# Feed-forward matmuls as two 64-column tiles, and each engine's order set by a plan made at build time

## The chip, the core and the metric

The kernel runs on one core of one Trainium2 chip. The metric is the device time in microseconds, the median of several executions. A profile of one execution gives the span from the first to the last instruction, and the busy time, waits and transfers of each engine: TensorE (PE, its weight loads as PEld), VectorE (DVE), ScalarE (ACT), GpSimd (POOL, which here only issues loads) and SyncE (SP, which issues the stores).

## The reference

Attention with a squared relu instead of a softmax, for 8 batches of 12 heads, 448 positions and 64 dimensions, and behind it one gated feed-forward layer on the 3,584 rows that come out:

```python
scores = scale * np.matmul(q, k.transpose(0, 1, 3, 2))
attn = np.maximum(scores, 0.0) ** 2 / S
attn_out = np.matmul(attn, v)
x = attn_out.transpose(0, 2, 1, 3).reshape(B * S, H * D)     # 3584 x 768
g = x @ w_gate                                               # 768 x 1536
gelu = 0.5 * g * (1.0 + erf(g * inv_sqrt2))
out = (gelu * (x @ w_val)) @ w_out                           # 1536 x 768
```

Inputs and output are float32 in memory; the kernel multiplies in bf16 and accumulates in float32.

## The kernel before

The work is cut by batch (8) and, in the attention, by pairs of heads (6 a batch, 48 in all). One pair n goes through four steps:

- `transposes(n)`: 16 PE transposes of 112 x 64 blocks of q and k into one PSUM bank (tile `tps`), in two 64-column halves of the array, one head in each; DVE copies the bank to `qkT`.
- `scores(n, half)`: two units of the four that a pair has. A unit is two matmuls side by side, each on 64 rows of the array, into a two-bank tile `sp`; ACT takes the relu into `rl`, DVE squares it into `attnT`.
- `values(n)`: 8 matmuls, two 64-column halves side by side, accumulate the pair's output in tile `op`; DVE scales it into `xT`.
- The batch's `xT` is full when its sixth pair is through.

The feed-forward works on a whole batch: `gate_value(b, fc)`, for 12 chunks of 128 of the 1,536 columns, accumulates six 448-column matmuls for the gate and six for the value, each on the full 128 x 128 array. ACT takes the gelu of the first, DVE multiplies it with the second into `uT`. `out_half(sb, t, g)` accumulates 12 matmuls of 384 columns for 128 rows of the output and half its width, ACT copies them to `osb`, and behind the second half SP stores them. Batches go two by two through `uT`, so an even batch has 6 such halves behind its chunks and an odd one 8.

The eight PSUM banks are split: one for `tps`, one for `op`, four for two `sp` tiles, two for the feed-forward's tile `ff`.

The order on every engine is the order in which the code is written. First come 48 warm-up matmuls of four tile shapes on a zero tile. Then stands the whole attention of batch 0, item by item: values of the pair before, transposes of the pair after, both score halves. From there on the feed-forward items of batch b are written one after the other, and the 12 attention items of batch b + 1 are dealt out between them at even shares of an estimated cost (`due`). POOL issues the loads: batch 0 in 18 pieces of one pair, then the weights with batch 1 in three parts between them, then each later batch whole, as soon as its buffer is free.

Of the kernel before, what the change touches and what calls it, by code (L numbers as in the profile page):

```python
# [8 lines left out]


@with_exitstack
def kernel(
# [10 lines left out]
    nc = tc.nc  # L23
# [9 lines left out]
    NP = B * NPAIR  # L33
    d_model, d_ff = moe_w_gate.shape
# [6 lines left out]
    WOG = 3  # L41

# [9 lines left out]
    apool = ctx.enter_context(tc.tile_pool(name="apool", bufs=10))  # L52
# [9 lines left out]

# [4 lines left out]


    def warm_up():
        full = psF.tile([128, 512], f32, name="ff", tag="F")  # L70
        cols = psF.tile([128, 512], f32, name="ff", tag="F")
        rows = psS.tile([128, 2, 512], f32, name="sp", tag="S")
        quad = psS.tile([128, 2, 512], f32, name="sp", tag="S")

        def mm(o, l, r, at):
            nc.tensor.matmul(o, l, r, start=True, stop=True, tile_position=at)  # L76

        for shape in ("full", "full", "cols", "full", "rows", "full", "quad", "cols", "rows"):
            for i in range(3):
                if shape == "full":  # L80
                    mm(full[:, :], warm[:, 0:128], warm[:, :], (0, 0))
                elif shape == "cols":
                    for j in range(2):
                        o = slice(64 * j, 64 * j + 64)
                        mm(cols[o, :], warm[:, o], warm[:, :], (0, 64 * j))
                elif shape == "rows":
                    for j in range(2):
                        r = slice(64 * j, 64 * j + 64)
                        mm(rows[:, j, :], warm[r, 0:128], warm[r, :], (64 * j, 0))
                else:  # L90
                    for j in range(4):
                        r = slice(64 * (j % 2), 64 * (j % 2) + 64)
                        o = slice(64 * (j // 2), 64 * (j // 2) + 64)
                        mm(quad[o, j % 2, :], warm[r, 0:64], warm[r, :],
                           (64 * (j % 2), 64 * (j // 2)))
# [5 lines left out]
          for i in range(FC // WOG)]  # L101

    def load_w12(i):
        cols = slice(i * WCH, (i + 1) * WCH)
        for wt, src in ((wg[i], moe_w_gate), (wv[i], moe_w_val)):
            nc.gpsimd.dma_start(
                wt[:, :, :], src[:, cols].rearrange("(c p) f -> p c f", p=128))

    def load_wo(i):
        rows = slice(i * WOG * 128, (i + 1) * WOG * 128)  # L110
        nc.gpsimd.dma_start(
            wo[i][:, :, :], moe_w_out[rows, :].rearrange("(c p) f -> p c f", p=128))

    batch = {}

    def alloc_batch(b):
        batch[b] = [qkv.tile([P, H, SC, D], bf16, name=n, tag=n) for n in ("q16", "k16", "v16")]

    def load_heads(b, h0, h1):
        for t, src in zip(batch[b], (q, k, v)):  # L120
            nc.gpsimd.dma_start(  # L121
                t[:, h0:h1, :, :],
                src[b, h0:h1].rearrange("h (p c) d -> p h c d", c=SC))


    qkT = {}
    att = {}
    xT = {}

    def transposes(n):  # L130
        b, pr = divmod(n, NPAIR)
        q16, k16, _ = batch[b]
        tps = psT.tile([128, 2, SC, 128], bf16, name="tps", tag="T")
        for c in range(SC):
            for i, src in enumerate((q16, k16)):
                for j in range(2):
                    rows = slice(64 * j, 64 * j + 64)
                    nc.tensor.transpose(tps[rows, i, c, 0:P], src[:, 2 * pr + j, c, :],  # L138
                                        ident[0:P, 0:P], tile_position=(0, 64 * j))
        qkT[n] = qk_pool.tile([128, 2, S], bf16, name="qkT", tag="qkT")  # L140
        nc.vector.tensor_copy(  # L141
            qkT[n].rearrange("d i (c p) -> d i c p", p=P), tps[:, :, :, 0:P])

    def scores(n, half):
        t = qkT[n]
        for c in (2 * half, 2 * half + 1):
            sp = psS.tile([128, 2, 512], f32, name="sp", tag="S")
            for j in range(2):
                rows = slice(64 * j, 64 * j + 64)
                nc.tensor.matmul(sp[0:P, j, 0:S], t[rows, 1, c * P:(c + 1) * P],  # L150
                                 t[rows, 0, :], start=True, stop=True,
                                 tile_position=(64 * j, 0))
            rl = rpool.tile([P, 2, S], bf16, name="rl", tag="rl")
            nc.scalar.activation(rl[:, :, :], sp[0:P, :, 0:S], AF.Relu)  # L154
            a = apool.tile([P, 2, S], bf16, name="attnT", tag="attnT")
            nc.vector.tensor_tensor(a[:, :, :], rl[:, :, :], rl[:, :, :], op=ALU.mult)  # L156
            att[n, c] = a

    def values(n):
        b, pr = divmod(n, NPAIR)  # L160
        v16 = batch[b][2]
        if pr == 0:
            xT[b] = xpool.tile([128, KC, S], bf16, name="xT", tag="xT")
        op = psO.tile([128, S], f32, name="op", tag="O")
        for c in range(SC):
            a = att.pop((n, c))
            for j in range(2):
                rows = slice(64 * j, 64 * j + 64)
                nc.tensor.matmul(op[rows, :], v16[:, 2 * pr + j, c, :], a[:, j, :],  # L169
                                 start=(c == 0), stop=(c == SC - 1),  # L170
                                 tile_position=(0, 64 * j))
        nc.vector.tensor_scalar_mul(xT[b][:, pr, :], op[:, :], scalar1=out_scale)  # L172

    def attn_item(m):
        n, half = divmod(m, 2)
        if half == 0:
            if n > 0:
                values(n - 1)
            if n + 1 < NP:
                transposes(n + 1)  # L180
            if n < NP:
                scores(n, 0)
        elif n < NP:
            scores(n, 1)


    uT = {}

    def gate_value(b, fc):
        x = xT[b]  # L190
        if b % 2 == 0 and fc == 0:
            uT[b // 2] = upool.tile([128, FC, 2 * S], bf16, name="uT", tag="uT")
        i, o = divmod(fc * 128, WCH)
        ps = []
        for w in (wg[i], wv[i]):
            pt = psF.tile([128, 512], f32, name="ff", tag="F")
            for dc in range(KC):
# [121 lines left out]
```

## Time and profile before

| | |
|---|---|
| median of 3 executions | 487.95 us (486.2 to 487.95) |
| the profiled execution | 487.95 us, its span 486.2 us |
| weight and input loads (POOL's queue) | 23.60 MB, 36.4% of 16 DMA engines |
| output stores (SP's queue) | 11.01 MB, 7.3% |
| score matmuls (L150) | 384, 396 ns each, 5.4 us of PE idle before them in all |
| relu on ACT (L154) | 192, 915 ns each |
| square on DVE (L156) | 192, 625 ns each |

A matmul's row in the profile lasts longer than its turn on PE, since matmuls are pipelined: what one costs is read from the start of one to the start of the next. Where two halves run side by side, a pair has one turn. The mean clock column tells which share of its full clock TensorE was granted.

### The profile page before, as it was taken

The numbers are of one execution on the slowest core, as the hardware profiler recorded it, in microseconds if no ns is written. First come the engines' busy times: TensorE is split into PE (matmuls) and PEld (weight loads), VectorE is DVE, ScalarE is ACT, GpSimd is POOL, SyncE is SP. The second block draws the span as 40 slices with busy tenths as digits, with TensorE's granted clock in tenths as the row PEclk, the third lists the DMA queues.
The fourth block names the chain that finished last, engine by engine and source line by source line (L and its number), as shares of the span: only waits on it lengthen the run. The fifth ranks groups of instructions, "written<-read, shape, count | busy, mean of one in ns | idle before, by whom it ended". The sixth has DMA issues, their size and how long they took to land.

```text
span 486.2 us, 8140 instructions
## 1 busy us (share of the span) xinstructions
PE 472.3 (97%) x3408; PEld 240.0 (49%) x3408; DVE 236.2 (49%) x385; ACT 238.8 (49%) x346; POOL 48.7 (10%) x67
## 2 busy tenths in 40 slices
PE   8788999999999999999999999999999999999996
PEld 2333444554555554555555554454455544555553
DVE  0666556445643466546563456536564466532210
ACT  1555654564545455555454645545455555452221
POOL 9744200100010000100010000100000000000000
PEclk9655999999999999999999999999999999999999
DMA  8999990950028600933009600555002200021013
GB/s 109 178 196 198 205 200 12 147 111 12 1 34 167 101 1 1 128 93 49 1 4 178 111 11 2 75 119 76 1 0 66 67 0 1 2 67 32 1 32 98
DMA packets 48501, 35.13 MB, mean 72 GB/s; under 512 B 1872, under 2 KB 44880, under 8 KB 48464
## 3 DMA queue, kind: packets, MB, share of 16 engines
q0 software_dynamic: 43984, 23.60, 36.4%
q1 hardware_dynamic: 4480, 11.01, 7.3%
q8 instruction: 26, 0.43, 0.4%
q14 instruction: 11, 0.09, 0.1%
HBM read 47.19 MB, written 11.01 MB: 120 GB/s over the span
## 4 chain that ended last, share of the span: by engine, by line
PE 94%; ACT 3%; DVE 2%; issue 1%; ACTq 0%
PE ff L198 46%; PE ff L218 23%; PE sp L150 10%; PE op L169 8%; PE tps L138 4%; ACT rl L154 2%; DVE attnT L156 2%; PE ff L76 1%; PE sp L76 0%; DVE qkT L141 0%; ACT osb L221 0%; DVE warm L64 0%; ACTq L154 0%
## 5 line engine op out<-in xcount | busy, mean ns | idle before, releaser
L154 ACT ACTIVATE rl<-sp 112x896 bf16<-112x896 f32 x192 | 165.1, 915 | 121.7 <-PE sp L150 121.7
L156 DVE TENSOR_TENSOR attnT<-rl 112x896 bf16<-112x896 bf16 x192 | 120.1, 625 | 103.1 <-ACT rl L154 103.1
L198 PE MATMUL ff<-xT,wg 128*128 128x448 bf16 x576 | 126.3, 356 | 0.0
L198 PE MATMUL ff<-xT,wv 128*128 128x448 bf16 x576 | 124.6, 352 | 0.0
L218 PE MATMUL ff<-wo,uT 128*128 128x384 bf16 x672 | 114.2, 326 | 0.0
L205 DVE TENSOR_TENSOR uT<-gel,ff 128x448 bf16<-128x448 bf16 x96 | 59.7, 622 | 76.7 <-PE ff L198 74.1
L218 PEld LDWEIGHTS <-uT 128*128 128x128 bf16 x672 | 63.8, 98 | 48.7 <-issue 8.1
L198 PEld LDWEIGHTS <-wg 128*128 128x128 bf16 x576 | 51.6, 98 | 63.0 <-issue 21.2
L198 PEld LDWEIGHTS <-wv 128*128 128x128 bf16 x576 | 56.4, 98 | 52.8 <-issue 0.4
L203 ACT ACTIVATE gel<-ff 128x448 bf16<-128x448 f32 x96 | 52.4, 546 | 57.5 <-PE ff L198 57.5
L150 PE MATMUL sp<-qkT 64*112 64x448 bf16 x384 | 62.1, 396 | 5.4 <-ACT rl L154 5.4
L221 ACT COPY osb<-ff 128x384 f32<-128x384 f32 x56 | 26.8, 479 | 63.3 <-PE ff L218 63.3
L169 PE MATMUL op<-attnT,v 112*64 112x448 bf16 x384 | 51.9, 382 | 2.0 <-DVE attnT L156 2.0
L172 DVE TENSOR_SCALAR xT<-op 128x448 bf16<-128x448 f32 x48 | 30.0, 625 | 38.4 <-PE op L169 38.4
L141 DVE COPY qkT<-tps 128x896 bf16<-128x896 bf16 x48 | 29.6, 617 | 11.4 <-PE tps L138 10.6
L169 PEld LDWEIGHTS <-v 112*64 112x64 bf16 x384 | 19.3, 112 | 30.9 <-issue 22.7
L150 PEld LDWEIGHTS <-qkT 64*112 64x112 bf16 x384 | 19.6, 131 | 30.0 <-issue 25.9
L121 POOL DMA_DIRECT2D q<-in_q_dram x15 | 12.0, 799 | 172.8 <-PE tps L138 169.3
L138 PE MATMUL tps<-ident,q 112*64 112x112 bf16 x384 | 27.0, 224 | 0.7 <-DVE qkT L141 0.7
L138 PE MATMUL tps<-ident,k 112*64 112x112 bf16 x384 | 27.0, 223 | 0.0
L138 PEld LDWEIGHTS <-q 112*64 112x64 bf16 x384 | 22.5, 117 | 4.3 <-issue 0.8
L138 PEld LDWEIGHTS <-k 112*64 112x64 bf16 x384 | 21.9, 118 | 3.9
(17 smaller groups left out, 52.5 us busy)
## 6 DMA issues: line engine op xcount, KB each, us to landing
q<-in_q_dram POOLq DMA_DIRECT2D x6, 672.0 KB, 7.0
k<-in_k_dram POOLq DMA_DIRECT2D x6, 672.0 KB, 10.3
v<-in_v_dram POOLq DMA_DIRECT2D x6, 672.0 KB, 8.1
out_dram<-osb SPq DMA_DIRECT2D x8, 336.0 KB, 3.2
wg<-in_moe_w_gate_dram POOLq DMA_DIRECT2D x6, 384.0 KB, 13.2
wv<-in_moe_w_val_dram POOLq DMA_DIRECT2D x6, 384.0 KB, 12.8
wo<-in_moe_w_out_dram POOLq DMA_DIRECT2D x4, 576.0 KB, 15.7
out_dram<-osb SPq DMA_DIRECT2D x8, 288.0 KB, 2.6
```

What stands on the lines that cost most here:

```text
L138: nc.tensor.transpose(tps[rows, i, c, 0:P], src[:, 2 * pr + j, c, :], ident[0:P, 0:P], tile_position=(0, 64 * j))
L141: nc.vector.tensor_copy(qkT[n].rearrange("d i (c p) -> d i c p", p=P), tps[:, :, :, 0:P])
L150: nc.tensor.matmul(sp[0:P, j, 0:S], t[rows, 1, c * P:(c + 1) * P], t[rows, 0, :], start=True, stop=True, tile_position=(64 * j, 0))
L154: nc.scalar.activation(rl[:, :, :], sp[0:P, :, 0:S], AF.Relu)
L156: nc.vector.tensor_tensor(a[:, :, :], rl[:, :, :], rl[:, :, :], op=ALU.mult)
L169: nc.tensor.matmul(op[rows, :], v16[:, 2 * pr + j, c, :], a[:, j, :], start=(c == 0), stop=(c == SC - 1), tile_position=(0, 64 * j))
L172: nc.vector.tensor_scalar_mul(xT[b][:, pr, :], op[:, :], scalar1=out_scale)
L198: nc.tensor.matmul(pt[:, 0:S], w[:, dc, o:o + 128], x[:, dc, :], start=(dc == 0), stop=(dc == KC - 1))
L203: nc.scalar.activation(gel[:, :], pt[:, 0:S], AF.Gelu)
L205: nc.vector.tensor_tensor(uT[b // 2][:, fc, base:base + S], gel[:, :], ps[1][:, 0:S], op=ALU.mult)
L218: nc.tensor.matmul(rp[:, 0:OGS], u[:, fc, cols], wo[i][:, o, g * OGS:(g + 1) * OGS], start=(fc == 0), stop=(fc == FC - 1))
L221: nc.scalar.copy(osb[0][:, g * OGS:(g + 1) * OGS], rp[:, 0:OGS])
```

## The change

Six things change together.

1. Every gate, value and output matmul is issued as two matmuls with 64 columns of weights each (`mm_cols`), at the tile positions (0, 0) and (0, 64), the form that the transposes and the values already have. They write the two halves of the partitions of one bank. The two score units of a half keep their form of two 64-row tiles.
2. The code no longer emits instructions as it goes. It makes lists of operations with an engine, a cost and dependencies, and `run_plan` emits them in the order in which they come ready: PE and POOL in the order of a list sorted by planned times, ACT and DVE whichever of the first 48 waiting operations could start first.
3. The planned times put batch 0 at 60 to 12 us ahead of the first feed-forward matmul, with the values of a pair 4.2 units behind its last scores; later batches are spread evenly over the feed-forward of the batch before and end 6 us ahead of it (`LEAD`).
4. Transposes, values and feed-forward share four banks (`psF`), with the two two-bank `sp` tiles beside them.
5. The warm-up is 10 pairs of one shape instead of 48 matmuls of four.
6. The three parts of batch 1 are loaded earlier among the weights, and there are 12 `attnT` buffers instead of 10.

The multiplications, the evictions and the bytes moved are the same.

```diff
+def run_plan(queues, pools, arrivals):
...
+        for e, ops in queues.items():
+            if at[e] < len(ops):
+                r = ready(ops[at[e]])
+                if r is not None:
+                    key = (max(r, free[e]), 0)
...
+        for e, ops in pools.items():
+            mine = None
+            for op in ops[:48]:
+                r = ready(op)
+                if r is not None:
+                    key = (max(r, free[e]), op.prio)
...
+        op.emit()
...
-    psT = ctx.enter_context(tc.tile_pool(name="psT", bufs=1, space=bass.MemoryType.PSUM))
-    psS = ctx.enter_context(tc.tile_pool(name="psS", bufs=2, space=bass.MemoryType.PSUM))
-    psO = ctx.enter_context(tc.tile_pool(name="psO", bufs=1, space=bass.MemoryType.PSUM))
-    psF = ctx.enter_context(tc.tile_pool(name="psF", bufs=2, space=bass.MemoryType.PSUM))
+    psS = ctx.enter_context(tc.tile_pool(name="psS", bufs=SB, space=bass.MemoryType.PSUM))
+    psF = ctx.enter_context(tc.tile_pool(name="psF", bufs=FB, space=bass.MemoryType.PSUM))
...
+    def mm_cols(o, lhsT, rhs, start, stop):
+
+        for j in range(2):
+            h = slice(64 * j, 64 * j + 64)
+            nc.tensor.matmul(o[h], lhsT[:, h], rhs, start=start, stop=stop,
+                             tile_position=(0, 64 * j))
...
+    def ring_dep():
+        return [ring[-FB]] if len(ring) >= FB else []
...
+            op = Op("PE", cost, emit, [t_op[n], relu_op.get(u - SB)],
+                    lag=0.25 if u < u1 - 1 else 0.15)
...
+        op = Op("PE", 0.77, emit, [head_op[b, pr, 2], *(sq_op[SC * n + c] for c in range(SC)),
+                                   *ring_dep()], lag=0.24)
...
-                nc.tensor.matmul(pt[:, 0:S], w[:, dc, o:o + 128], x[:, dc, :],
-                                 start=(dc == 0), stop=(dc == KC - 1))
+                mm_cols(pt[:, 0:S], w[:, dc, o:o + 128], x[:, dc, :],
+                        dc == 0, dc == KC - 1)
...
-            nc.tensor.matmul(rp[:, 0:OGS], u[:, fc, cols],
-                             wo[i][:, o, g * OGS:(g + 1) * OGS],
-                             start=(fc == 0), stop=(fc == FC - 1))
+                mm_cols(rp[:, 0:OGS], u[:, fc, t * TT:(t + 1) * TT],
+                        wo[i][:, o, g * OGS:(g + 1) * OGS], fc == 0, fc == FC - 1)
...
+    LEAD = 6.0
+    for b in range(B):
+        if b == 0:
+            lo, hi = -60.0, -12.0
+        elif b == 1:
+            lo, hi = -8.0, starts[1] - LEAD
+        else:
+            lo, hi = starts[b - 1] - LEAD, starts[b] - LEAD
+        step = (hi - lo) / (SC * NPAIR)
+        for pr in range(NPAIR):
+            n = NPAIR * b + pr
+            work.append((lo + (SC * pr) * step - max(3.0, 2 * step), 1, add_transposes, (n,)))
+            work.append((lo + (SC * pr + SC - 1) * step + max(4.5, (4.2 if b == 0 else 3.3) * step), 2, add_values, (n,)))
+        for u in range(0, SC * NPAIR, SB):
+            work.append((lo + (u + SB - 1) * step, 3, add_scores,
+                         (SC * NPAIR * b + u, SC * NPAIR * b + u + SB)))
+    work.sort(key=lambda w: w[:2])
```

How the instructions now stand is seen at three places. The first is DVE's queue at the start, in batch 0, where PE's scores and values wait for it. A row is one operation, or several in a row with their count; `qkT` is the copy of a pair's transposes, `attnT` a square, `xT` the scaled values. Before:

```order
L141 COPY qkT<-tps 128x896 x2
L156 TENSOR_TENSOR attnT<-rl 112x896 x4
L172 TENSOR_SCALAR xT<-op 128x448
L141 COPY qkT<-tps 128x896
L156 TENSOR_TENSOR attnT<-rl 112x896 x4
```

and in the changed kernel:

```order
L205 COPY qkT<-ff 128x896 x2
L233 TENSOR_TENSOR attnT<-rl 112x896 x4
L205 COPY qkT<-ff 128x896
L233 TENSOR_TENSOR attnT<-rl 112x896 x3
L262 TENSOR_SCALAR xT<-ff 128x448
L233 TENSOR_TENSOR attnT<-rl 112x896
L205 COPY qkT<-ff 128x896
```

The first scaled values stand behind seven squares instead of four, and the third pair's transposes are copied ahead of them: the values of a pair have moved one pair back.

The second place is PE's queue at the end of a value accumulation, where the values of a pair follow it (batch 1, while batch 0 is in the feed-forward). `wv` and `v` are weights loaded into the array, and the shape is that of the output. Before:

```order
L198 LDWEIGHTS wv_113
L198 MATMUL ff<-xT,wv_113 128x448
L169 LDWEIGHTS v_127
L169 MATMUL op<-attnT,v_127 64x448
L169 LDWEIGHTS v_127
```

and in the changed kernel:

```order
L136 LDWEIGHTS wv_106
L136 MATMUL ff<-xT,wv_106 64x448
L136 LDWEIGHTS wv_106
L136 MATMUL ff<-xT,wv_106 64x448
L257 LDWEIGHTS v_340
L257 MATMUL ff<-attnT,v_340 64x448
```

The last accumulation step is now two matmuls of 64 output partitions, and the values behind it have the same shape and the same tile positions.

The third place is POOL's queue behind the 18 loads of batch 0, where the first weights and the first part of batch 1 (four heads, two pairs: 112 x 4 x 256) are issued. Before:

```order
L106 DMA wg_106<-in_moe_w_gate_dram 128x6x256
L106 DMA wv_112<-in_moe_w_val_dram 128x6x256
L106 DMA wg_107<-in_moe_w_gate_dram 128x6x256
L106 DMA wv_113<-in_moe_w_val_dram 128x6x256
L121 DMA q_125<-in_q_dram 112x4x256
L121 DMA k_126<-in_k_dram 112x4x256
```

and in the changed kernel:

```order
L160 DMA wg_100<-in_moe_w_gate_dram 128x6x256
L160 DMA wv_106<-in_moe_w_val_dram 128x6x256
L175 DMA q_316<-in_q_dram 112x4x256
L175 DMA k_334<-in_k_dram 112x4x256
L175 DMA v_340<-in_v_dram 112x4x256
L160 DMA wg_101<-in_moe_w_gate_dram 128x6x256
L160 DMA wv_107<-in_moe_w_val_dram 128x6x256
L160 DMA wg_102<-in_moe_w_gate_dram 128x6x256
```

The first part of batch 1 has moved ahead of the second pair of weights; its second part now stands behind the third pair instead of the fourth, its third part behind the fourth instead of behind half of `w_out`.

More of the change, by code (lines that the diff above doesn't have):

```diff
@@ L66 @@
     ctx.enter_context(tc.manual_schedule())
[L69 to L95, printed above, removed]
+    def mm_cols(o, lhsT, rhs, start, stop):
[3 more added lines that the diff above has]
+                             tile_position=(0, 64 * j))
+    PE, ACT, DVE, POOL = [], [], [], []
+    arrivals = {}
     wg = [wpool.tile([128, KC, WCH], bf16, name=f"wg{i}", tag=f"wg{i}") for i in range(NW)]
@@ L144, in scores @@
[L144 to L157, printed above, removed]
@@ L159, in values @@
-    def values(n):
-        b, pr = divmod(n, NPAIR)
[L161 to L172, printed above, removed]
@@ new lines, in load_heads, with emit @@
+    def load_heads(b, h0, h1, deps=((), (), ())):
+        for i, (name, src) in enumerate((("q16", q), ("k16", k), ("v16", v))):
+            def emit(i=i, name=name, src=src):
+                if (b, i) not in batch:
+                    batch[b, i] = qkv.tile([P, H, SC, D], bf16, name=name, tag=name)
+                nc.gpsimd.dma_start(
+                    batch[b, i][:, h0:h1, :, :],
+                    src[b, h0:h1].rearrange("h (p c) d -> p h c d", c=SC))
+            op = load(4 * (h1 - h0) * S * D, emit, deps[i])
+            for pr in range(h0 // 2, h1 // 2):
+                head_op[b, pr, i] = op
@@ L292 @@
+    work.sort(key=lambda w: w[:2])
+    add_warm_up(10)
+    for _, _, fn, args in work:
+        fn(*args)
+        b, pr = divmod(args[0], NPAIR)
+        if fn is add_values and pr == NPAIR - 1 and b + 2 < B:
+            n = args[0]
+            load_heads(b + 2, 0, H, ((t_op[n],), (t_op[n],), (o_op[n],)))
+    run_plan({"PE": PE, "POOL": POOL}, {"ACT": ACT, "DVE": DVE}, arrivals)
 _INS = ['q', 'k', 'v', 'moe_w_gate', 'moe_w_val', 'moe_w_out']
```

302 lines of the change are left out of this document (196 added, 106 removed).

## The prediction, made before the changed kernel was run

> **What bounds the kernel now.** I read the page first, for the busiest engine and the chain that ended last; then a table by stage; then the chain and the timeline inside the two stages that differ.
>
> ```profile
> span 486.2 us, 8140 instructions
> PE 472.3 (97%) x3408; PEld 240.0 (49%) x3408; DVE 236.2 (49%) x385; ACT 238.8 (49%) x346; POOL 48.7 (10%) x67
> PE 94%; ACT 3%; DVE 2%; issue 1%; ACTq 0%
> ```
>
> PE is 94% of the chain, so only two things can shorten this kernel: less PE time, or fewer microseconds in which PE isn't the bound. The table by stage (stretch, its length, then busy time of PE, PEld, DVE, ACT, POOL with counts, granted clock, DMA share, GB/s) says where the latter lie.
>
> ```profile
> 6.60:16.85 10.25, 7.44 (x82) 3.04 (x83) 3.75 (x6) 3.34 (x4) 10.25 (x16) 1.00 1.30 165
> 16.85:50.95 34.10, 28.86 (x188) 13.66 (x188) 21.21 (x34) 19.07 (x23) 16.54 (x22) 0.50 1.41 195
> 51.00:438.50 387.50, 387.50 (x2887) 198.53 (x2885) 202.82 (x332) 204.66 (x299) 16.28 (x18) 1.00 0.37 63
> 438.58:481.50 42.92, 42.92 (x240) 23.33 (x240) 8.08 (x13) 9.89 (x19) 0.00 (x0) 1.00 0.13 37
> 481.50:486.20 4.70, 0.02 (x1) 0.00 (x0) 0.00 (x0) 0.48 (x1) 0.00 (x0) 0.82 0.28 84
> ```
>
> From 51 to 481.5 us PE is never idle, at full clock; DVE and ACT are busy half the time. The last 4.7 us are the last eviction and its store. Before 51 us PE has only 188 matmuls in 34 us, at clock 0.50. The chain there (start, length, what):
>
> ```profile
> 28.73 0.58 PE op L169 x2
> 29.32 0.75 PE tps L138 x16
> 30.06 0.57 PE sp L150 x2
> 31.47 0.92 ACT rl L154
> ...
> 34.04 0.64 DVE attnT L156
> 34.72 0.58 PE op L169 x2
> ...
> 48.95 3.40 PE ff L198 x12
> ```
>
> and ACT's row of the timeline in the same loop:
>
> ```profile
> 36.65 3.35 ACT L154 ACTIVATE rl<-sp 112x896 bf16<-112x896 f32 x4 [2.63 <-PE sp L150]
> ```
>
> One head pair takes 34.72 − 28.73 = 5.99 us, and ACT idles 2.63 us in each: its next scores stand on PE behind values that wait for the last square of the same pair. So batch 0 runs as a serial loop PE, ACT, DVE, PE, and the first feed-forward matmul starts at 48.95. Call that point F.
>
> **After F.** I write T for the transposes of a pair, S for two score units, V for the values of a pair, G and U for a gate and a value accumulation, R for one output half. The steady rows of the timeline (start, length, then what; the length holds the latency of the last one, so costs are read from start to start), and two of the chain at the end, where nothing disturbs:
>
> ```profile
> 201.73 2.12 PE L218 MATMUL ff<-wo,uT 128*128 128x384 bf16 x12
> 203.79 0.95 PE L169 MATMUL op<-attnT,v 112*64 112x448 bf16 x8
> 204.57 0.22 PE L138 MATMUL tps<-ident,q 112*64 112x112 bf16 x2
> ...
> 205.06 0.59 PE L150 MATMUL sp<-qkT 64*112 64x448 bf16 x4
> 205.58 4.07 PE L218 MATMUL ff<-wo,uT 128*128 128x384 bf16 x24
> 209.58 0.58 PE L150 MATMUL sp<-qkT 64*112 64x448 bf16 x4
> ...
> 221.06 1.30 PE L198 MATMUL ff<-xT,wg 128*128 128x448 bf16 x6
> 222.20 1.30 PE L198 MATMUL ff<-xT,wv 128*128 128x448 bf16 x6
> 223.43 0.95 PE L169 MATMUL op<-attnT,v 112*64 112x448 bf16 x8
> ```
>
> ```profile
> 438.58 27.35 PE ff L198 x144
> 465.92 15.61 PE ff L218 x96
> ```
>
> Undisturbed, a 448-column matmul costs 27.35/144 = 0.190 us and a 384-column one 15.61/96 = 0.163. G to U is 1.14 us (6 x 0.19), but U to V is 1.23 and R12 to V 2.06 instead of 1.95: a change between the full array and 64-column tiles costs some 0.10. T after V follows without such a step (0.78 for four pairs of V, 0.195 a pair), T to S has one (0.49 for 16 transposes, 8 x 0.05 plus 0.10), S takes 0.52, R24 after it 4.00 instead of 3.90. Per pair there are five changes: into V, into and out of S, twice.
>
> **The change, part by part.** (1) *64-column tiles in G, U and R.* V, T, G, U and R now share one tile shape, so the change into V goes: 0.10, and some 0.02 that V's first pair loses (0.78 − 4 x 0.19), 0.12 a pair. 42 of the 48 V stand behind F: **−5.0 us**. The four changes around S stay. Every full matmul becomes two half-width ones, 1,824 pairs. V's pairs cost 0.195 with that first loss in it, 0.19 without; I take 0.19, so **0**. At 0.195 the 1,152 pairs of G and U cost 5.8 us and the 672 of R some 3.4: upper end +9. Below 0 nothing, since the columns streamed are the same.
>
> This needs the weight loads to hide. Full loads already do. A half one is no shorter (the groups' last numbers ahead of the second bar are mean ns):
>
> ```profile
> L198 PEld LDWEIGHTS <-wg 128*128 128x128 bf16 x576 | 51.6, 98 | 63.0 <-issue 21.2
> L169 PEld LDWEIGHTS <-v 112*64 112x64 bf16 x384 | 19.3, 112 | 30.9 <-issue 22.7
> ```
>
> Two of 112 ns in turn would be 0.224 us, more than the 0.19 of the pair above them, yet V and T run at 0.19 and 0.05 a pair with two loads each: the loads overlap. The Trainium skill speaks against the change here: "TensorEngine Tiling (Array Packing)", Restrictions and Gotchas, excludes Fast Weight Load under column tiling, and "TensorE: Matmul & The Clock Gate", Part 3, lets a load overlap a running matmul only in another row group, while both tiles here use all rows. The 112 ns for half the columns fit the first; T's pairs of 0.05 us disagree with the second. By these pages the loads would show and the time would be that of the third rival.
>
> (2) *The head.* The new order puts V one pair behind its scores, so nothing on PE waits for a square just made. What is late next: ACT and DVE at once. ACT's four relus take 3.35 us, (3.35 − 0.92)/3 = 0.81 apart. DVE, back to back:
>
> ```profile
> 67.34 0.62 DVE L205 TENSOR_TENSOR uT<-gel,ff 128x448 bf16<-128x448 bf16 x1 [2.05 <-PE ff L198]
> 67.88 0.62 DVE L172 TENSOR_SCALAR xT<-op 128x448 bf16<-128x448 f32 x1
> 68.42 0.61 DVE L141 COPY qkT<-tps 128x896 bf16<-128x896 bf16 x1
> ```
>
> That is 0.54 an operation, six a pair: 3.24 us, the same as four relus. The rows of the start, and of three loads with the us from issue to landing:
>
> ```profile
> 1.19 5.55 PE L76 MATMUL ff<-warm 128*128 128x512 bf16 x15 [1.19 <-DVE warm L64]
> 2.42 0.67 POOL L121 DMA_DIRECT2D k<-in_k_dram  x1
> k<-in_k_dram POOLq DMA_DIRECT2D x1, 112.0 KB, 3.7
> 21.09 0.83 POOL L106 DMA_DIRECT2D wv<-in_moe_w_val_dram  x1 [1.40 <-DMA wg<-in_moe_w_gate_dram]
> wv<-in_moe_w_val_dram POOLq DMA_DIRECT2D x1, 384.0 KB, 13.2
> 48.10 0.77 POOL L111 DMA_DIRECT2D wo<-in_moe_w_out_dram  x1 [1.25 <-DMA wg<-in_moe_w_gate_dram]
> wo<-in_moe_w_out_dram POOLq DMA_DIRECT2D x1, 576.0 KB, 18.0
> ```
>
> The warm row holds 12 slots of 512 columns in 5.55 us, 0.46 each; ten end at 5.8, and the first k lands at 2.42 + 3.7 = 6.1. From the first transpose to the first relu I allow 2.4 us: 8.5. Then 24 relus: 19.4 us if neither engine ever misses a beat, 21.6 at 0.90; I take 0.90, as two equally loaded engines fed in order will miss some: 30.1. Behind the last relu stand a square, V, its copy and the scores of the next pair: 2.5. F = 32.6. But the eighth pair's transposes stand only 3 us behind F (G, U, one S) and need a k that is loaded after the third weight pair. The bytes ahead of it are those that landed with wv at 21.09 + 13.2 = 34.3, plus two 224 KB loads, 2.3 us at 195 GB/s: 36.6. So F counts as no earlier than 33.6 whatever the engines do. I take **34.5**, a gain of 14.4. The lower end is 33.6; the upper is the first rival. One more S stands ahead of F, which is 0.6 less behind it. The 2 us after F at half clock, which lost 1.0, go if the head keeps full clock.
>
> (3) *Load order.* Weights 2 to 6 land up to 3.5 us later (three 224 KB loads); they are wanted one pair every 4.5 us from F on. All w_out has the same bytes ahead as before and lands at 66.1; the first R is 37 us behind F, at 71. Batch 2 (two 672 KB loads, 73) is wanted 41 us behind F, at 75. **0**, with 2 to 5 us of cover; if F came earlier the cover would go first. SP's stores are not moved.
>
> (4) *Four shared banks, planned ACT and DVE queues.* Each buffer is taken again four accumulations later, over 2 us, against evictions of 0.6 us on engines half idle: **0**, up to +5 (0.1 a pair) if an eviction stands behind squares.
>
> Sum: −14.4 − 5.0 − 0.6 − 1.0 = −21.0. The profiled execution took 487.95 us, the span and 1.75 around it, and is the median of the runs shown: **467.0**.
>
> **Rivals.** *Cold head.* Clock 0.50 held although PE was busy 28.9 of 34.1 us. If the short warm-up, ending before the first load lands, doesn't bring full clock, or the new head can't keep it, PE bounds the head: per pair at half clock T 0.75, V and S 1.5 each (four 448-column pairs, by the 0.75 of eight 112-column ones), four changes of 0.18: 4.5 against 3.6. F near 38.3, the 1.0 lost again: **472**. For it: the old stage stayed cold 85% busy. Against: the new order packs PE fuller. The Trainium skill ("TensorE: Matmul & The Clock Gate", HAM oscillation) wants only that no idle gap exceeds about 3.4 us, by which the head would be warm; here the clock fell at 16.85 although PE idles only 2.8 us in all of the 10.25 before, so the rule doesn't decide.
>
> *No gain behind F.* G to V costs what U to V costs now, because 128 and 112 rows differ (never adjacent in this trace), or the shared banks take 5 us: **472**.
>
> *Weights show.* The slower end: half-width pairs above 0.19 us, in G, U and R, by loads or by the doubled stream of instructions. All the gain is gone at 21/1,824 = 11.5 ns a pair; two exposed loads of 112 ns would be +409, **876**. Against: V and T, 1,152 matmuls already in this form.
>
> *The change doesn't do what it says.* The head stays serial through some wait of the new queues: only the steady gain, **482**.
>
> **How the numbers follow.** Forecast 0.50, cold head 0.26, no gain behind F 0.11 (with both 477), pairs at 0.195 (476) 0.05, serial head 0.03, weights showing 0.04 with nearly all of it slower, 0.01 even. A measurement of this kernel tells about 0.5% from no change, so faster 0.95, same 0.01, slower 0.04. The range must take in both clocks and the ends 33.6 and +5: 463.5 to 475.
>
> **What would show it.** In the changed profile: a first feed-forward matmul near 34.5 at clock 1.00 (cold head: 0.50, at 38); relus under 0.95 us apart before it; the eighth pair's transposes waiting for a load of k or not at all; G and U at 1.14 us with V behind at no extra; PE idle 0 from F to 42.9 us before the last eviction. Half-width pairs above 0.195 us, or PE waiting for DVE behind F, would make the prediction wrong.

## The result, and the profile after

| | median | lowest to highest | runs |
|---|---|---|---|
| before, measured beside it | 487.07 us | 485.56 to 487.95 | 4 |
| after | 467.99 us | 467.05 to 468.14 | 4 |

The ratio is 0.9607, with a 95% interval of 0.9575 to 0.9639. The profiled execution of after took 467.05 us, its span 465.3: 20.9 less than the span of 486.2 before, where the sum of the prediction said 21.0. These two executions are the slowest of before and the fastest of after; by the medians of the table the gain is 19.1 us, and the forecast of 467.0 lies 1.0 below the median of 467.99.

The page of the changed kernel: span, busy time of each engine, and the engines' shares of the chain that ended last.

```profile
span 465.3 us, 11773 instructions
PE 453.7 (98%) x5204; PEld 261.5 (56%) x5204; DVE 232.5 (50%) x385; ACT 237.6 (51%) x346; POOL 48.5 (10%) x67
...
PE 91%; DMA 5%; POOL 3%; issue 0%; ACT 0%; POOLq 0%
```

DMA is new in the chain with 5% and POOL, which issues the loads, with 3%; DVE and ACT have left it. The table by stage of after (columns as in the prediction: stretch, length, busy time of PE, PEld, DVE, ACT, POOL, granted clock, DMA share, GB/s) shows where PE is now idle:

```profile
9.53:16.36 6.83, 6.29 (x42) 2.70 (x43) 5.61 (x11) 5.46 (x7) 6.83 (x11) 0.50 1.38 179
16.36:33.08 16.72, 13.28 (x158) 6.84 (x157) 14.71 (x28) 15.00 (x19) 9.33 (x13) 1.00 1.41 188
33.08:460.60 427.52, 427.28 (x4954) 248.94 (x4952) 210.92 (x347) 213.67 (x318) 23.84 (x27) 1.00 0.41 70
460.60:465.30 4.70, 0.08 (x2) 0.00 (x0) 0.00 (x0) 0.48 (x1) 0.00 (x0) 0.81 0.28 84
```

The half-clock stretch of 34.1 us has shrunk to 6.8. F, the start of the first feed-forward matmul, is 33.08 instead of 48.95, and from there to the last matmul PE is idle 0.24 us in all. ACT and DVE are busy about 90% of the 16.7 us before F, as equals: they bound that stage now, up to F. ACT's row there (start, length, count of relus without a gap) shows it for ACT:

```profile
15.97 13.59 ACT L229 ACTIVATE rl<-sp 112x896 bf16<-112x896 f32 x16 [0.83 <-PE sp L224]
```

Sixteen relus stand (13.59 − 0.92)/15 = 0.845 us apart; before, four of them were followed by 2.63 us of nothing.

What limits the start once the engines no longer do is read from the chain of after (start, length, what) and from PE's row of the timeline around F:

```profile
23.15 0.28 issue
23.43 12.99 DMA k<-in_k_dram
36.42 0.04 issue
36.46 0.54 PE ff L200 x14
```

```profile
33.08 1.32 PE L136 MATMUL ff<-xT,wg 128*64 128x448 bf16 x12
34.23 1.30 PE L136 MATMUL ff<-xT,wv 128*64 128x448 bf16 x12
35.47 0.59 PE L224 MATMUL sp<-qkT 64*112 64x448 bf16 x4
35.98 0.24 PE L200 MATMUL ff<-ident,q 112*64 112x112 bf16 x2
36.46 0.24 PE L200 MATMUL ff<-ident,k 112*64 112x112 bf16 x2 [0.24 <-DMA k<-in_k_dram]
...
36.83 1.30 PE L136 MATMUL ff<-xT,wg 128*64 128x448 bf16 x12
37.97 1.30 PE L136 MATMUL ff<-xT,wv 128*64 128x448 bf16 x12
39.10 0.93 PE L257 MATMUL ff<-attnT,v 112*64 112x448 bf16 x8
```

The load of k for the eighth pair lands at 36.42, and the transposes that want it (L200) start there. The first transposes of q and of k start 36.46 − 35.98 = 0.48 us apart, where 0.07 is usual (19.69 and 19.76 for an earlier pair). Without the wait they would have come some 0.4 us sooner, so F counts as 33.5 rather than 33.08. Two more things are seen in these rows. U to V is 39.10 − 37.97 = 1.13 us, against 1.23 before: the change of form into V is gone. And G to U is 1.14 to 1.15 with twelve half-width matmuls, as it was with six full ones, though a half-width load is no shorter:

```profile
L136 PEld LDWEIGHTS <-wg 128*64 128x64 bf16 x1152 | 60.2, 109 | 53.7 <-issue 18.6
```

So the 20.9 us have two parts: 48.95 − 33.08 = 15.9 in the head, and 432.64 − 427.61 = 5.0 between F and the end of the last matmul.

### The profile page after: what moved, and what is told of

Read it like the earlier page. It is cut to its first block, busy times and chain, and to the rows that moved or that the text cites. A ratio compares the mean times of both kernels' runs of the same rounds, so it can differ in the third digit from the quotient of the medians.

```text
span 465.3 us, 11773 instructions
## 1 busy us (share of the span) xinstructions
PE 453.7 (98%) x5204; PEld 261.5 (56%) x5204; DVE 232.5 (50%) x385; ACT 237.6 (51%) x346; POOL 48.5 (10%) x67
## 4 chain that ended last, share of the span: by engine, by line
PE 91%; DMA 5%; POOL 3%; issue 0%; ACT 0%; POOLq 0%
PE ff L136 72%; PE sp L224 9%; PE ff L257 7%; PE ff L200 3%; DMA k<-in_k_dram 3%; DMA q<-in_q_dram 2%; POOL q L175 1%; POOL v L175 1%; POOL k L175 1%; POOL wg L160 0%; POOL wv L160 0%; ACT osb L324 0%; POOL ident masks.py:199 0%; POOL ident masks.py:197 0%; POOLq masks.py:199 0%
## 5 line engine op out<-in xcount | busy, mean ns | idle before, releaser
L136 PE MATMUL ff<-xT,wg 128*64 128x448 bf16 x1152 | 126.4, 355 | 0.0
L136 PE MATMUL ff<-xT,wv 128*64 128x448 bf16 x1152 | 125.0, 352 | 0.0
L136 PE MATMUL ff<-wo,uT 128*64 128x384 bf16 x1344 | 117.3, 327 | 0.0
L136 PEld LDWEIGHTS <-uT 128*64 128x64 bf16 x1344 | 73.9, 110 | 39.4 <-issue 7.8
L136 PEld LDWEIGHTS <-wg 128*64 128x64 bf16 x1152 | 60.2, 109 | 53.7 <-issue 18.6
L136 PEld LDWEIGHTS <-wv 128*64 128x64 bf16 x1152 | 65.3, 110 | 43.7
L257 PE MATMUL ff<-attnT,v 112*64 112x448 bf16 x384 | 45.2, 358 | 0.0
L224 PEld LDWEIGHTS <-qkT 64*112 64x112 bf16 x384 | 18.9, 126 | 38.4 <-issue 33.6
L205 DVE COPY qkT<-ff 128x896 bf16<-128x896 bf16 x48 | 29.8, 621 | 12.2 <-PE ff L200 12.0
L262 DVE TENSOR_SCALAR xT<-ff 128x448 bf16<-128x448 f32 x48 | 30.0, 624 | 11.6 <-PE ff L257 10.2
L200 PE MATMUL ff<-ident,k 112*64 112x112 bf16 x384 | 24.9, 214 | 1.1 <-DMA k<-in_k_dram 1.1
L200 PE MATMUL ff<-ident,q 112*64 112x112 bf16 x384 | 25.6, 216 | 0.0
L257 PEld LDWEIGHTS <-v 112*64 112x64 bf16 x384 | 19.2, 111 | 10.2 <-issue 1.8
L200 PEld LDWEIGHTS <-q 112*64 112x64 bf16 x384 | 20.4, 111 | 5.7 <-issue 2.0
L200 PEld LDWEIGHTS <-k 112*64 112x64 bf16 x384 | 19.9, 111 | 4.5 <-DMA k<-in_k_dram 1.9
```

What stands on the lines that cost most here:

```text
L136: nc.tensor.matmul(o[h], lhsT[:, h], rhs, start=start, stop=stop, tile_position=(0, 64 * j))
L200: nc.tensor.transpose(t[h, i, c, 0:P], batch[b, i][:, 2 * pr + j, c, :], ident[0:P, 0:P], tile_position=(0, 64 * j))
L205: nc.vector.tensor_copy(qkT[n].rearrange("d i (c p) -> d i c p", p=P), box[0][:, :, :, 0:P])
L224: nc.tensor.matmul(sp[0:P, j, 0:S], t[r, 1, c * P:(c + 1) * P], t[r, 0, :], start=True, stop=True, tile_position=(64 * j, 0))
L257: nc.tensor.matmul(o[h, 0:S], batch[b, 2][:, 2 * pr + j, c, :], a[:, j, :], start=(c == 0), stop=(c == SC - 1), tile_position=(0, 64 * j))
L262: nc.vector.tensor_scalar_mul(xT[b][:, pr, :], box[0][:, 0:S], scalar1=out_scale)
```

## The experiments

My theory after the result: the head gains by the order of its work alone, up to where a load of k lands; behind F the gain is the changes of tile form that are no longer there; and the four shared banks cost nothing because there are four of them. The rivals: the head gains by its clock; the half-width matmuls are themselves faster, or hide a loss; the banks don't matter. Diffs are against after, where nothing else is said.

### The 64-column tiles: taken out, and put in alone

`e1_full` keeps order, banks and loads, and makes every feed-forward matmul a full one again (the warm-up alone keeps its pairs):

```diff
-        for j in range(2):
-            h = slice(64 * j, 64 * j + 64)
-            nc.tensor.matmul(o[h], lhsT[:, h], rhs, start=start, stop=stop,
-                             tile_position=(0, 64 * j))
+        nc.tensor.matmul(o, lhsT, rhs, start=start, stop=stop)
```

> Part 1 alone is undone: gate, value and output products are single matmuls on the full array again, the new order, banks, loads and warm-up stay. My theory (a change of tile form costs about 0.1 us, and the half-width pairs cost what full matmuls do): behind the first feed-forward matmul F the new order has 80 places at which transposes or values meet the feed-forward (28 + 17 into them, 35 out of them), each 0.096 us plus some 0.01 to 0.02 for the first matmul behind it, less 0.01 at each of 79 places behind scores: +7.6 us, so 475 to 476 us; PE idle nowhere behind F. Rival (half-width pairs are dearer, by weight loads or twice the instructions, and the gain is all in the head): no change or faster than 468.

Measured: 475.09 us (474.47 to 475.25), ratio to before 0.9758 [0.9735, 0.9781]. F is 33.35. The table by stage behind it, and U and V of its timeline:

```profile
33.36:468.80 435.44, 435.18 (x3130) 215.07 (x3128) 212.61 (x346) 213.65 (x318) 23.85 (x27) 1.00 0.40 68
```

```profile
38.36 1.30 PE L134 MATMUL ff<-xT,wv 128*128 128x448 bf16 x6
39.59 0.95 PE L254 MATMUL ff<-attnT,v 112*64 112x448 bf16 x8
```

U to V is 1.23 again, and PE is 435.44 − 427.52 = 7.9 us longer behind F. That is more than the 5.0 of the result, because the new order parts V and T from each other: counted in the timelines behind F, form changes are 209 before, 164 in after and 244 here. The 7.9 us over 80 changes are 0.099 each.

The half-width matmuls are not free everywhere, and this run shows it. By the differences of the starts, G takes 1.159 us to U behind a group of scores in after (57 places), and 1.146 here; an output half in the same place takes 0.013 more as well (23 places). That is 1.1 us in all, already taken off in the 7.9.

`e4_before_cols` is the kernel before with this one part of the change (gate and value; the output likewise):

```diff
-                nc.tensor.matmul(pt[:, 0:S], w[:, dc, o:o + 128], x[:, dc, :],
-                                 start=(dc == 0), stop=(dc == KC - 1))
+                for j in range(2):
+                    h = slice(64 * j, 64 * j + 64)
+                    nc.tensor.matmul(pt[h, 0:S], w[:, dc, o + 64 * j:o + 64 * j + 64], x[:, dc, :],
+                                     start=(dc == 0), stop=(dc == KC - 1),
+                                     tile_position=(0, 64 * j))
```

> The kernel before with one part of the change alone: gate, value and output products as two 64-column matmuls; order, banks, head, loads and warm-up as before. My theory: 43 changes into values go, 0.096 us each, and 0.9 us that the first pair of values lost; 0.8 is given back at the first pair behind scores: -4.2 us, 482 to 484 us, PE idle nowhere behind F. Rival (tiles pay only with the new order, or cost): 487 us or more.

Measured: 484.0 us (482.42 to 484.18), ratio 0.9937 [0.9913, 0.9962]. By the timeline 166 changes are left, 43 fewer, and behind F:

```profile
48.30:476.50 428.20, 428.20 (x4958) 255.48 (x4956) 211.97 (x346) 216.35 (x320) 16.95 (x19) 1.00 0.35 62
```

F to the end of the last matmul is 428.38 instead of 432.64, so 4.3 us less. Some 0.4 of them are clock: the half clock ends sooner behind F here, and the first G, cold in both, takes 1.79 us to U (48.23 to 50.02) against 2.17 before (48.88 to 51.05). The other 3.9 us over 43 changes are 0.09 each. By the medians the whole kernel gains only 2.4 us, 484.0 against 486.41 of the kernel before measured beside it, with executions 1.8 us apart for this kernel and 2.4 for the one before; the per-change price rests on the traces. The two kernels agree on it, 0.09 and 0.10 net of the small loss behind scores, and how many changes are saved depends on the order.

### The load order, and the clock in the head

`e2_old_loads` goes back to the load order of before:

```diff
-    load_heads(1, 0, 4)
     load_w12(1)
+    load_heads(1, 0, 4)
     load_w12(2)
-    load_heads(1, 4, 8)
     load_w12(3)
-    load_heads(1, 8, 12)
+    load_heads(1, 4, 8)
     load_w12(4)
     load_w12(5)
...
+    load_wo(0)
+    load_wo(1)
+    load_heads(1, 8, 12)
```

> The load order of before, all else as in the changed kernel. My theory: F's real bound is the k of batch 1's second part, for which the eighth pair's transposes wait at 36.46 us; in the old order that k landed at 40.7, so these transposes wait until then and everything behind them moves: +4.2 us, 472 us, with about 4.5 us of PE idle at that one place. Rival (the engines bound the head, loads are hidden): within 1 us of 468.

Measured: 472.88 us (470.2 to 472.98), ratio 0.9701 [0.9668, 0.9735]; F 33.42. The timeline behind F:

```profile
35.81 0.58 PE L224 MATMUL sp<-qkT 64*112 64x448 bf16 x4
39.70 0.24 PE L200 MATMUL ff<-ident,q 112*64 112x112 bf16 x2 [3.30 <-DMA q<-in_q_dram]
40.87 0.30 PE L200 MATMUL ff<-ident,k 112*64 112x112 bf16 x2 [0.93 <-DMA k<-in_k_dram]
```

The eighth pair's transposes wait 3.30 us for q and 0.93 for k, and from 40.46, within the second wait, to 43.87 the granted clock is 0.50. With the old loads a part of the head's gain would have been a new wait 3 us later. The earlier load is needed for the gain, not a gain of its own.

`e5_fill` adds ten dummy matmuls to the first 9 us, where PE waits for loads, so that nothing disturbs the clock:

```diff
+    fill = {(add_transposes, 0): 3, (add_scores, 0): 2}
...
+        if fill.get((fn, args[0])):
+            add_warm_up(fill.pop((fn, args[0])))
```

> The changed kernel with ten more dummy matmuls (five pairs on the zero tile) in the two places where PE waits in the first 9 us, so that the clock isn't lost at 9.5 us. My theory (the k of the eighth pair bounds the head, not the engines): the head runs at full clock, F comes 1 to 1.5 us earlier, near 32, and the eighth pair's transposes still start at 36.4, now after a wait of some 1.5 us: no change, 467.5 to 468.5 us. Rival (the engines bound the head, the load is a coincidence): 1 to 1.5 us faster.

Measured: 467.14 us (466.81 to 467.33), ratio 0.9583 [0.9565, 0.9602], 0.85 under after's median and between what was expected and what the rival said. The interval overlaps after's, so the medians alone don't tell the two kernels apart. The table by stage of the profiled execution shows the clock now full throughout the head (its mean clock is 0.998, that of the other three executions 0.993 to 0.995, so they may have lost it for a while):

```profile
6.00:34.00 28.00, 22.23 (x261) 11.21 (x256) 23.31 (x42) 23.99 (x29) 19.72 (x28) 1.00 1.39 183
```

F comes a microsecond sooner, at 32.07, and the same load takes it back: the eighth pair's k is waited for 0.92 us, and those transposes start at 36.22, where after has 36.46.

`e6_fill_loads` therefore moves the second part of batch 1 one weight pair forward as well (`load_heads(1, 4, 8)` ahead of `load_w12(2)`).

> The same dummy matmuls, and batch 1's second part loaded ahead of the third weight pair instead of behind it, so that its k lands some 4 us earlier, near 32.5. My theory: neither bound is left where it was; the eighth pair's transposes start near 35 without a wait, 1.3 to 1.9 us faster than the changed kernel, 466 to 467 us. Rival (clock or load alone would do): the same time as the run with dummy matmuls alone.

Measured: 467.38 us (465.38 to 469.39), ratio 0.9589 [0.9561, 0.9616]: the expected gain is not in the median. The profile shows no wait for k any more, but also a clock of 0.50 from 11.53 to 18.35, in spite of the dummies, and F at 33.61. The five executions differ in the same thing: mean clock 1.000 gave 465.38 us, 0.993 gave 467.2 to 467.5, and 0.985 gave 469.39. So it seems that the head of these kernels stands at the edge of a clock that some executions lose for a while, and what the load alone is worth stays within that scatter. The one execution at full clock is 1.8 us under e5's median, and 2.6 under after's, where 1.3 to 1.9 were expected; one execution doesn't prove it, and the point stays open.

### The order of the head

`e3_serial_head` puts the values of batch 0's pairs right behind their own scores again, as the kernel before had them:

```diff
-... + max(4.5, (4.2 if b == 0 else 3.3) * step), 2, add_values, (n,)))
+... + (0.1 if b == 0 else max(4.5, 3.3 * step)), 2, add_values, (n,)))
```

> In batch 0 alone the values of a pair stand right behind its own scores again (planned 0.1 units behind instead of 4.2); all else as in the changed kernel. My theory (the head was slow because PE's next scores stood behind values that wait for the last square): four relus 3.35 us, then a square, two matmuls of values and the next scores before ACT goes on, 5.1 us a pair at full clock and up to 5.6 at half, against 3.42: F 8 to 11 us later, 476 to 479 us, ACT idle some 1.7 us in each pair. Rival (the head's gain comes from the start 4 us earlier and from the clock): F at most 3 us later, 471 us or less.

Measured: 479.47 us (478.82 to 479.59), ratio 0.9847 [0.9824, 0.987], half a microsecond above what was expected. F is 44.94. ACT's row of the timeline, and the stage:

```profile
24.98 3.54 ACT L229 ACTIVATE rl<-sp 112x896 bf16<-112x896 f32 x4 [1.89 <-PE sp L224]
30.41 3.54 ACT L229 ACTIVATE rl<-sp 112x896 bf16<-112x896 f32 x4 [1.89 <-PE sp L224]
```

```profile
8.01:44.94 36.93, 33.14 (x214) 13.75 (x214) 22.20 (x38) 22.52 (x27) 23.99 (x34) 0.50 1.42 191
```

Four relus, then a gap: the picture of the kernel before, with 5.43 us a pair instead of 5.99, and the clock at half. So is it the serial order that makes the head long, or the half clock that comes with it? `e10_serial_warm` keeps the serial order and puts eight dummy matmuls in the gap of each pair, ahead of its values:

```diff
+        if fn is add_values and args[0] < NPAIR:
+            add_warm_up(4)
```

> The serial head of the earlier run (values right behind their own scores in batch 0) with four pairs of dummy matmuls ahead of each pair's values, in PE's wait for the last square, so that PE is busier and may keep full clock. My theory (the order makes the head long, the half clock is its consequence): 4.9 to 5.1 us a pair at full clock against 5.43 without and 3.42 in the changed order, F at 40 to 43, 474 to 477 us. Rival (the half clock made the head long): near the changed order's pace once the clock is full, F below 37, 471 us or less.

Measured: 475.07 us (474.11 to 476.58), ratio 0.9754 [0.9725, 0.9784]. The clock is full from 13.6 on, and F is 41.50. One turn of its chain:

```profile
22.93 0.38 PE ff L257 x2
23.32 0.52 PE sp L224 x4
23.83 0.53 PE ff L200 x16
24.36 0.02 issue
24.39 0.62 DVE qkT L205
25.01 1.08 DVE attnT L233 x2
26.09 0.00 issue
26.09 0.94 ACT rl L229
27.03 0.02 issue
27.06 0.64 DVE attnT L233
27.69 0.04 issue
27.73 0.38 PE ff L257 x2
```

Values, scores and transposes on PE, the copy and two squares on DVE, the last relu on ACT, its square and again values follow each other through three engines, 27.73 − 22.93 = 4.80 us a pair at full clock, against about four relus of 0.845, 3.4 us, in after. The dummy matmuls are not in this chain. Taken in this order, the steps split the 15.9 us of the head: 48.95 to 44.94 for what e3 still has of the change (0.56 less in each of six pairs is 3.4 of these 4.0), to 41.50 for the clock, to 33.08 for values one pair behind their scores. The last step, 8.4 us, is the largest, and with it the clock comes back without any dummies but for the 6.8 us at its start.

### The four banks, and a version with two

`e11_two_banks` gives the shared ring two banks instead of four:

```diff
-    FB = 4
+    FB = 2
```

> The changed kernel with two shared banks instead of four, scores in groups of two as they are, all else the same. My theory (the four banks are what lets transposes and values stand anywhere): at 37 places transposes follow a feed-forward accumulation and values follow them; the values then need the bank of the accumulation before the transposes, evicted 0.75 to 0.9 us after its end, and the transposes cover 0.4: 0.35 to 0.5 us each, +15 us, 481 to 485 us. Rival (two banks are enough, as before the change): within 1 us of 468.

Measured: 486.79 us (486.39 to 487.38), ratio 0.9994 [0.9983, 1.0006]; everything the change gained is gone. F is 33.27, as in after, and it is 446.74 us from there to the last matmul. PE's waits (in total, times, longest):

```profile
PE ff L257 <- DVE uT L295: 9.8, 25, 0.4
...
PE ff L257 <- ACT osb L324: 1.6, 9, 0.2
```

V (L257) waits for the eviction of U or of an output half, since T stands between them: at these 25 + 9 = 34 places T takes the one bank and V wants the one that the accumulation before T had. From the start of T to the start of V it is 0.95 us in the first 25 and 0.74 in the other 9, against 0.40 in after: 0.50 us a place, 17 us in all, more than the idle time alone. Three places where an output half follows T cost another 1.0. Behind F the kernel is 446.74 − 427.61 = 19.1 us longer where 15 were expected; the price was too small, the mechanism is the expected one.

Two banks in the ring leave room for three `sp` tiles, hence three score units in a row instead of two, and a third fewer form changes. Four kernels tried that. `e7_three` (`SB = 3`, `FB = 2`, `LEAD = 8`, values one unit later) and `e8_all` (the same with the dummies of e5 and the loads of e6) left T and V wherever the planned times put them:

> Scores in groups of three units instead of two: three sp tiles on six banks, so that transposes, values and feed-forward share two banks instead of four; values and the end of each batch's attention are planned one unit and 2 us later behind them. My theory (what is left behind F is changes of tile form, about 0.1 into a group of scores, 0.04 for its first unit, 0.1 out of it): 55 groups behind F instead of 82, 27 x 0.245 = 6.6 us less, one unit more: 461 to 462 us if two banks are enough, up to 465 if evictions then hold PE. Rival (four shared banks carry the change): PE waits for DVE or ACT behind F, 468 us or more.

> Groups of three, the dummy matmuls and the earlier load of batch 1's second part together. My theory: the gains add, 460 to 461 us; where the two banks hold PE at the start of the feed-forward, 462 to 464.

Measured: 474.9 us (474.18 to 476.75), ratio 0.9737 [0.9718, 0.9757], and 473.38 us (472.76 to 475.61), ratio 0.9722 [0.9698, 0.9746]; both missed by about 10. The timeline of e7 shows why:

```profile
46.84 1.30 PE L136 MATMUL ff<-xT,wv 128*64 128x448 bf16 x12
47.98 0.22 PE L200 MATMUL ff<-ident,q 112*64 112x112 bf16 x2
...
48.93 1.33 PE L136 MATMUL ff<-xT,wg 128*64 128x448 bf16 x12 [0.39 <-DVE uT L295]
```

U, then T, then G: T lasts 0.4 us, and G wants the bank of U, which DVE has only just begun to evict. It is e11's wait with another victim, and I had priced the missing banks at 0 to 3 us.

`e9_grouped` sets T right ahead of a group of scores and V right behind one, so that an accumulation of 1.1 us or a group of 0.7 stands between two uses of a bank:

```diff
+        if fn is add_transposes:
+            before = [g for g in groups if g <= when]
+            when = before[-1] if before else when
+        else:
+            behind = [g for g in groups if g >= when]
+            when = behind[0] if behind else when
```

> Groups of three score units on six banks and two banks for the rest, as in the run before, but each pair's transposes are planned right ahead of a group of scores and each pair's values right behind one, the attention of a batch ends 11 us ahead of its feed-forward, and batch 1's second part is loaded ahead of the third weight pair. My theory (two banks held PE because transposes of 0.4 us alone between two accumulations left the eviction of the one before 0.5 us short; with 1.1 us of scores behind them nothing is short): PE idle nowhere behind F, 54 groups instead of 82, 28 x 0.245 = 6.9 us less than the changed kernel behind F, the head up to 2 us longer: 461 to 464 us. Rival (two banks are too few in any order): 468 us or more.

Measured: 470.55 us (469.65 to 470.9), ratio 0.9656 [0.9632, 0.968]. That is in the rival's range, but not for the rival's reason: the waits for banks are gone, but for one of 0.9 us right behind F, and a wait for loads has come instead:

```profile
63.61 1.30 PE L136 MATMUL ff<-xT,wv 128*64 128x448 bf16 x12
69.49 0.31 PE L200 MATMUL ff<-ident,q 112*64 112x112 bf16 x2 [4.58 <-DMA q<-in_q_dram]
72.65 0.30 PE L200 MATMUL ff<-ident,k 112*64 112x112 bf16 x2 [2.86 <-DMA k<-in_k_dram]
```

```profile
72.70:77.27 4.57, 4.57 (x34) 2.36 (x36) 2.03 (x4) 2.53 (x3) 0.00 (x0) 0.50 1.45 198
```

Batch 2's first transposes had moved to 64.8 us, some 8 us ahead of their data, by the larger lead and by rounding to the group before. PE waits 7.4 us; the clock falls at 67.03, during the wait, and stays at half until 77.27. `e12_grouped_late` plans batch 2's attention 10 us later and leaves its first two T unrounded, and likewise values that would fall right ahead of a batch's feed-forward:

```diff
-            lo, hi = starts[b - 1] - LEAD, starts[b] - LEAD
+            lo, hi = starts[b - 1] - (1.0 if b == 2 else LEAD), starts[b] - LEAD
```

> The grouped run, with one thing mended: the attention of batch 2 is planned 10 us later, since its first transposes stood at 64 us on PE and waited for q and k until 72.7 (7.7 us), and the clock fell to half behind that wait (another 2.3). My theory: those 10 us go and the fewer changes of tile form show: 460 to 463 us, PE idle behind F under 2 us. Rival (two banks or fewer, larger groups cost what they save): 468 us or more.

Measured: **461.75 us** (461.32 to 462.47), ratio 0.9483 [0.947, 0.9495]. It is faster than both kernels. Its page, and the stage behind F (F is 34.94 here, so the stretch begins a microsecond ahead of it):

```profile
span 460.7 us, 11739 instructions
PE 447.3 (97%) x5204; PEld 276.6 (60%) x5204; DVE 223.2 (48%) x385; ACT 238.6 (52%) x346; POOL 48.7 (11%) x67
```

```profile
33.90:456.10 422.20, 421.05 (x4954) 262.82 (x4949) 201.60 (x346) 214.76 (x318) 23.40 (x27) 1.00 0.41 70
```

There are 54 groups of scores behind F instead of 82, so 108 form changes instead of 164, and F to the last matmul falls from 427.61 to 421.16 us. The 56 changes at 0.10 are 5.6 of these 6.45; the rest I haven't traced.

## Why the prediction held, step by step

**64-column tiles: right in kind, 1.6 too much in sum.** The prediction took off 5.0 for the change into V, 0.6 for the score group that moved ahead of F and 1.0 for the half clock behind it, 6.6 in all; 5.0 were measured behind F. The terms that it named hold. Between before and e4, by the differences of the starts, U to V falls from 1.228 to 1.135 us and V itself from 0.781 to 0.758, together 0.116 where 0.12 was expected, 4.9 at 42 places; one group of scores fewer stands behind F (82 against 83); and the half clock there is gone. What failed is a term put at nothing, that of the half-width pairs: they cost 0.19 but for the first behind a group of scores, where 0.013 is lost at each of 80 places, 1.1 in all (e1 and e4 both show it). The wait for k and what goes with it costs another 0.4: F to the last matmul is 427.61 us in after and 427.18 in e6, where nothing waits for k. These two make up the difference. The expected 0.19 for a pair elsewhere held, and the rival "weights show", with its chance of 0.04, did not come: 1,824 pairs, two loads of some 110 ns each, PE never idle for them. What the Trainium skill says of loads under running matmuls ("TensorE: Matmul & The Clock Gate", Part 3: only in another row group) doesn't agree with these rows, since both tiles use all rows.

**The head: right in what bounds it, about 1 us too late.** The engines alone were put at 32.6 and came to 33.08, with two errors that partly cancel: the first relu starts at 7.79 instead of 8.5 and the 24 relus take 21.8 us to 29.56, as expected (21.6), but from there to F it is 3.5 us instead of 2.5, since a T and a second S stand there as well. The load of k was put at 36.6 and landed at 36.42, so by the prediction's own rule, 3 us ahead of the landing, F counts as 33.4. The prediction had this at 33.6 and chose 34.5, above both bounds: its lower end would have been the better choice. That the order does most of it and the clock 3.4 us is shown by e10 beside e3. Relus 0.845 apart lie between the 0.81 without any miss and the 0.90 chosen; that the mean of all 24 is at 0.90 is owed to the first eight, which the half clock and the start hold up.

**Load order: 0 as a price, but not idle.** No weight was waited for. e2 shows what the prediction left unsaid: the lower end of F rested on the new order of the loads, and with the old one the kernel is some 5 us slower.

**Four banks and planned queues: 0, as said.** e11 shows the cover: it is the number of banks. No run takes the planned ACT and DVE queues, the shorter warm-up or the two more `attnT` buffers out by themselves, so what each is worth isn't shown. With two, the same places cost 17 us, more than the bound of 5 that the prediction kept for them with four.

**The rivals.** The cold head came for 6.8 us instead of for the whole stage, and cost little: with the dummies of e5 F is 1.0 us sooner, and the median 0.85, which is within the intervals. Of the other rivals none was seen: the gain behind F is there, the weights don't show, and the head is not serial. The error of +1.5 us in the head's gain and that of −1.6 behind F cancel, so the span agrees better than its parts.

## What to carry to other kernels

Read the stage in which PE isn't the bound first: a step that waits for an engine's answer to work just issued belongs one unit of work later, and what is then late next is often a load, so look at the queue's order together with the engines'. Where matmuls of several tile forms alternate, give them one form, or put those that need another form in longer groups, and multiply the number of changes by the measured price of one before building anything. A ring of accumulators needs enough banks for the shortest operation in it: a 0.4 us user between two long ones makes two banks behave like one.

## What the runs showed of the hardware

- A change of tile form costs PE 0.09 to 0.10 us in both orders (3.9 us for 43 in e4, 7.9 for 80 in e1). A half-width accumulation right behind scores costs 0.013 us more than a full one (1.159 against 1.146 us from G to U, after and e1).
- Column tiles of the same rows hide two weight loads of 109 to 110 ns under pairs that take turns of 0.19 us, for whole kernels (e4, after).
- The granted clock drops in stretches near multiples of 3.41 us: 3.41 in e2, 6.83 in after, 10.24 in e9. In e2 and e9 it fell while PE waited for loads (waits of 4.2 and 7.4 us), in e9 2.1 us after the row of PE's last matmul had ended (64.91 to 67.03). In e3 it stayed at half with PE busy 33.14 of 36.93 us. Between executions of one kernel the mean clock differs: in e6 it was 1.000 in the fastest (465.38 us) and 0.985 in the slowest (469.39 us).
